# Second batch's first pair turned by the DMA crossbar, fp32 sums ahead of relus, GpSimd casts in another order

## The chip, the cores and the metric

The kernel runs on one NeuronCore of a Trainium2 chip. Five engines work beside each other, each through its own instructions in order: TensorE (PE; its weight loads are listed as PEld), VectorE (DVE), ScalarE (ACT), GpSimd (POOL) and SyncE (SP), which here only starts DMAs. They wait for each other through semaphores. The metric is the device time of one execution in microseconds (us). Before the change it is 285.78 us, the median of four executions from 285.17 to 286.19.

## What is computed

A block-sparse attention over 4 batches of 8 heads, 768 positions and 64 features, and behind it a mixer with a low-rank step over the positions and a two-layer network over the features:

```python
def _attn_ref(q, k, v, sampled_blocks):
    scores = scale * np.matmul(q, k.transpose(0, 1, 3, 2))
    ...                                   # mask: neighbour, edge and sampled blocks of 32
    scores = np.where(mask, scores, -1000000000.0)
    scores = scores - np.max(scores, axis=-1, keepdims=True)
    attn = np.exp(scores)
    attn = attn / (np.sum(attn, axis=-1, keepdims=True) + 1e-09)
    return np.matmul(attn, v).astype(np.float32)

def _moe_ref(x, U, V, w_ch1, w_ch2):
    xt = x.transpose(0, 2, 1)
    h = xt @ U @ V                        # U: 768 x 32, V: 32 x 768
    u = x + h.transpose(0, 2, 1)
    ch = np.maximum(u @ w_ch1, 0.0) @ w_ch2    # 512 x 2048, 2048 x 512
    return (u + ch).astype(np.float32)
```

x is the attention's output with the heads side by side: 4 x 768 x 512.

## The kernel before

**Tiling.** Two heads make a pair, `i` = 0 to 15, four pairs to a batch. Positions are six tiles of 128. A pair's scores are made in nine *units*, `u` = 0 to 8: `scores` (L464) writes one unit into a PSUM tile `psc` of 128 x 1024, ScalarE exponentiates it into `est` (L481), and the values (`pav`) are summed from the nine `est` tiles. Reciprocal and product on VectorE give `xs` (fp32); a cast gives `xh` (fp16). The mixer then makes `pa` from `xh` and U, casts it to `a`, makes `ph` from `a` and V, adds `xs` to get `xf` (fp32), casts that to `uh` (fp16) and turns it into `uT`. The network reads `uT`: `pt` = w1 x `uT`, a relu to `tT` (fp16), `pch` = `tT` x w2, and the sum with `xf` is stored.

**Queries and keys** are loaded by SP in fp32 (`qld`, `kld`), cast by GpSimd to `qst`, `kst` (`cast`, L235), and then turned so that the features lie on the partitions. This is done in one of two ways: by TensorE transposes into a PSUM tile `pturn` and a VectorE copy out of it (`turn_part`, L918), or by a DMA through the crossbar started on SP (`turn_dma`, L261). `qst`, `kst` and the turned `qT`, `kT` have two buffers each.

**The first batch** (pairs 0 to 3) is an order written by hand. The loop at L1025 makes the scores of a unit, then the values of the unit three before it (`flush_value`), then calls `at_unit(i, u)` (L945), which places everything else: loads, casts, the turns of the next pair (`turn_part(i + 1, ...)`), the mask, the weight loads issued by GpSimd (`WLOADS`) and the mixer's steps of the pair before (`tails`). Here the mask is added inside the score product, through one-hot rows in `qa` and `ka`. In pair 0 (L977 to L1005) GpSimd casts U, V and then pair 2's q, k, v.

**From the second batch on** a planner orders the work while the kernel is built. It keeps a clock for each engine (`clk`), lists of due tasks (`later`, `run_engines`) and a list of w1/w2 steps of the batch before (`fill`, `run_fill`); scores are multiplied by a 0/1 mask on VectorE (L502). A relu may go to ScalarE or VectorE, whichever its clocks say is free first. `unit_sides` (L1043) turns pair `i + 1` by the crossbar at unit 0 of pair `i`, for `i` over 4: the crossbar so begins with pair 6.

**The head between the two** (L1078 to L1115) is written out. The first three units of pair 4 are made beside the end of batch 0; their masks wait in `early`. The last pair's `xs` and `xf` in fp32 are put off (`put_off`), so that the fp16 forms that feed `uT` come first. Then come eight short w1 steps, of which five are each followed by `run_engines(1e9)`, which places all due relus; then the fp32 sums; then two more PSUM double tiles are opened (`more_doubles`); then pair 5 is turned by TensorE (L1109 to L1111).

Of the kernel before, what the change touches and what calls it, by code (L numbers as in the profile page):

```python
# [21 lines left out]
def kernel(  # L22
# [12 lines left out]
    nc = tc.nc  # L35

    B, H, S, D = q.shape
    BLK = 32
    NB = S // BLK
    T = S // P  # L40
    HD = H * D
    HP = H // 2
    R = moe_U.shape[1]
# [54 lines left out]
    keep = tc.keep_in_program_order  # L98
# [5 lines left out]
    clk = {"pe": 0.0, "act": 0.0, "dve": 0.0, "pool": 0.0}  # L104
# [30 lines left out]
    def later(eng, first, fn, when=None):  # L135
        count[0] += 1
        when = clk["pe"] if when is None else when
        tasks[eng].append((when + LAG, first, count[0], fn))

    def run_engines(t):  # L140
        while True:
            best = None
            for eng in ("act", "dve"):
                for kind in (eng, "any"):
                    for task in tasks[kind]:
                        start = max(clk[eng], task[0])
                        late = 0.15 if kind == "any" and eng == "dve" else 0.0
                        key = (start + late, task[1], task[2])
                        if start <= t and (best is None or key < best[0]):
                            best = (key, eng, kind, task, start)  # L150
            if best is None:
                return
            _, eng, kind, task, start = best
            tasks[kind].remove(task)
            clk[eng] = start
            clk[eng] += task[3](eng)

    def more_doubles(tag, n):
        first[tag].__exit__(None, None, None)
        pool = ctx.enter_context(  # L160
            tc.tile_pool(
                name=f"double{n}p", bufs=1, space=bass.MemoryType.PSUM,
                side="left" if tag == "ps" else "right",
            )
        )
        doubles[n] = (pool, clk["pe"])
# [38 lines left out]
    Ut = wpool.tile([P, T, P], FP16)  # L205
    Vt = wpool.tile([P, T, P], FP16)
# [22 lines left out]
    def issue(i, names="qkv"):  # L229
        if i >= NPAIR:  # L230
            return
        for nm in names:
            keep(nc.sync.dma_start(out=new_ld(i, nm), in_=src_of(nm, i)))

    def cast(i, nm):  # L235
        if i >= NPAIR:
            return
        b, hp = divmod(i, HP)
        ld = lds.pop((i, nm))
        if nm == "v":  # L240
            keep(
                nc.gpsimd.tensor_copy(  # L242
                    out=vts[b % 2][:, 2 * hp : 2 * hp + 2, :, 0:D], in_=ld
                )
            )
            return
        st = stpool.tile([P, T, 2, D], FP16, tag="st" + nm, name=nm + "st")
        keep(nc.gpsimd.tensor_copy(out=st.rearrange("p t h d -> p h t d"), in_=ld))  # L248
        sts[i, nm] = st
# [11 lines left out]
    def turn_dma(i, nm):  # L261
        if i >= NPAIR:
            return
        st = sts.pop((i, nm))
        qkT[i, nm] = qkpool.tile([P, T, P], FP16, tag=nm + "T", name=nm + "T")
        keep(
            nc.sync.dma_start_transpose(
                out=qkT[i, nm], in_=st.rearrange("p t h d -> p (t h d)")
            )
        )  # L270
# [647 lines left out]
    def turn_part(i, nm, part):  # L918

        if part == 0:  # L920
            turning[nm] = pst_tile([P, T, P], FP16, "pturn", tag="ps")
        turn_some(sts[i, nm], turning[nm], 3 * part, 3 * part + 3)
        if part == 1:
            del sts[i, nm]
            pt = turning.pop(nm)
            if i < HP:
                dst = {"q": qa, "k": ka}[nm][i % 2]
                for h in range(2):
                    half_copy(nc.vector.tensor_copy, dst, h, pt, 0, T)
            else:  # L930
                qkT[i, nm] = qkpool.tile([P, T, P], FP16, tag=nm + "T", name=nm + "T")
                keep(nc.vector.tensor_copy(out=qkT[i, nm], in_=pt))
            run_on("dve", 0.48)
# [8 lines left out]
    }  # L942


    def at_unit(i, u):  # L945
        if (i, u) in MASKS:
            mask_tiles(MASKS.index((i, u)))
        if i == 0:
            if u == 0:
                warm_pe(1)  # L950
                turn_some(qst, pq, TQ, T)
                turn_some(kst, pk, TK, T)
                for h in range(2):
                    mask_rows("dve", h, pm2[:, 0, 0:QB], QA, S)
                    keep(
                        nc.sync.dma_start(
                            out=qa[1][h][mrows[h], :], in_=qa[0][h][mrows[h], :]
                        )
                    )
                    hot_rows(nc.sync, 1, h, D)  # L960
                for nm, o, pt, t in (("q", qa[0], pq, TQ), ("k", ka[0], pk, TK)):
                    for h in range(2):
                        half_copy(nc.vector.tensor_copy, o, h, pt, t, T)
                for h in range(2):
                    keep(nc.sync.dma_start(out=mvld[h * R : h * R + R], in_=moe_V))
                keep(
                    nc.sync.dma_start(
                        out=uld, in_=moe_U.rearrange("(p t) r -> p (t r)", t=T)
                    )
                )  # L970
                issue(2, "qk")
                cast(1, "q")
                cast(1, "k")
                cast(1, "v")
            if u == 1:
                issue(2, "v")
            if u == 3:  # L977
                for r in range(2):
                    at = r * R
                    keep(  # L980
                        nc.gpsimd.tensor_copy(
                            out=Ut[rows[r]].rearrange("p t (h c) -> p t h c", h=2)[
                                :, :, :, at : at + R
                            ],
                            in_=uld[rows[r]]
                            .rearrange("p (t r) -> p t r", t=T)[:, :, None, :]
                            .broadcast_to([D, T, 2, R]),
                        )
                    )
                keep(  # L990
                    nc.gpsimd.tensor_copy(
                        out=Vt[0 : 2 * R, :, :],
                        in_=mvld.rearrange("r (p t) -> r t p", t=T),
                    )
                )
                issue(3)
            if u == 6:
                cast(2, "q")
                cast(2, "k")
                cast(2, "v")  # L1000
            if u == 4:
                turn_part(1, "q", 0)
                turn_part(1, "q", 1)
            if u in (5, 6):
                turn_part(1, "k", u - 5)  # L1005
            return
        if u == 0:
            issue(i + 3)
        if i == 2 and u == 0:
            for h in range(2):  # L1010
                keep(nc.sync.dma_start(out=Vd[rows[h]], in_=Vt[rows[0]]))
        if (i, u) in WLOADS:
            WLOADS[i, u]()
        if u in (1, 2, 3, 4):
            turn_part(i + 1, "qk"[(u - 1) // 2], (u - 1) % 2)
        if u == 6:
            cast(i + 2, "q")
            cast(i + 2, "k")
        if u == 8:
            cast(i + 2, "v")  # L1020
        for _ in range({0: 1, 5: 2, 6: 1, 7: 1}.get(u, 0)):
            if tails:
                tails.popleft()()
# [48 lines left out]
    def run_fill():  # L1072
        cost, fn, kind = fill.popleft()
        fn()
        state["last"] = clk["pe"]
        return cost
# [3 lines left out]
    for gi in range(3):  # L1080
        next_unit(True)
        if gi == 0:
            flush_value()
            tails.popleft()()
            flush_value()
        if gi == 1:
            flush_value()
            put_off.pop(0)()
        if gi == 2:
            tails.popleft()()  # L1090
            tails.popleft()()
            put_off.pop(0)()


    fill.extend(mlp_steps(0))
# [4 lines left out]
    tails.popleft()()  # L1100
    run_fill()
    tails.popleft()()
    for _ in range(5):
        run_fill()
        run_engines(1e9)
    while put_off:
        put_off.pop(0)()
    more_doubles("pav", 2)
    for nm in "qk":  # L1109
        for part in range(2):  # L1110
            turn_part(HP + 1, nm, part)  # L1111
    clk["pe"] = clk["dve"] = max(clk["act"], clk["pe"])
    more_doubles("ps", 3)
    for mask in early:
        later("dve", 3, mask, 0.0)  # L1115

    opened, credit = 1, 0.0
    uT_at = {b: [] for b in range(B)}
# [115 lines left out]
```

## Time and profile before

| what | value |
|---|---|
| median of 4 executions | 285.78 us |
| profiled execution | 285.17 us, its span 283.4 us |
| granted TensorE clock | 0.999 |
| exps on ScalarE (L481) | 144, 142.5 us, 1030 ns each |
| w1 and w2 matmuls | 95.6 and 93.4 us busy |
| mask products on VectorE (L502) | 108, 834 ns each |
| transposes by the crossbar | 12 of uT, 10 of qT, 10 of kT |
| bytes moved by DMA | 37.2 MB, 131 GB/s on average |

The profile is that of one execution on the chip. A row of a timeline gives the start, the duration, the engine, the line and the operation, what it writes and reads, and how many instructions were merged; in brackets stands the idle time before it and what ended it. The duration of matmuls is modelled and contains a latency, so the distance from start to start says what one costs. Times count from the start of the span.

### The profile page before, as it was taken

What the parts mean: (1) busy time and instruction counts of PE and PEld (TensorE: products, weight loads), DVE (VectorE), ACT (ScalarE), POOL (GpSimd) and SP (SyncE); (2) the same over time, 40 slices, a digit from 0 to 9 for tenths busy, and PEclk for the clock granted to TensorE, in tenths of its full rate; (3) what the DMA queues carried; (4) which work ended last, traced back from release to release, by engine and by line L of the source; (5) the groups of instructions that cost most, each with busy time, mean ns of one, the idle gap of its engine ahead of it and who ended that gap; (6) DMA issues with size and microseconds to landing.
All of it is one profiled execution on the core that took longest, in us unless ns stands there. A gap on an engine that the chain in (4) does not pass through costs nothing.

```text
span 283.4 us, 8067 instructions
## 1 busy us (share of the span) xinstructions
PE 275.4 (97%) x3509; PEld 164.9 (58%) x3509; DVE 182.5 (64%) x285; ACT 178.5 (63%) x201; POOL 85.4 (30%) x102
## 2 busy tenths in 40 slices
PE   8999999799999999999999999999999999999996
PEld 3477775456565656656656464656565654565443
DVE  5667767866979898986876959886768551000112
ACT  3799996397969676584894757496868200665000
POOL 2578854103345353341332525151102011000000
PEclk9999999999999999999999999999999999999999
DMA  6999999916264695656154574912100303100112
GB/s 171 275 320 301 238 259 268 251 30 197 56 200 49 191 214 200 137 192 160 41 119 133 124 205 120 169 30 58 30 2 2 102 10 97 75 0 2 74 74 75
DMA packets 45235, 37.20 MB, mean 131 GB/s; under 512 B 27144, under 2 KB 42832, under 8 KB 45200
## 3 DMA queue, kind: packets, MB, share of 16 engines
q1 hardware_dynamic: 42024, 32.26, 41.4%
q0 software_dynamic: 2688, 4.19, 8.0%
q8 instruction: 27, 0.44, 0.7%
q10 hardware_dynamic: 488, 0.24, 0.3%
q14 instruction: 8, 0.07, 0.1%
HBM read 27.90 MB, written 6.29 MB: 121 GB/s over the span
## 4 chain that ended last, share of the span: by engine, by line
PE 83%; ACT 12%; DVE 2%; issue 1%; DVEq 0%
PE pch L174 29%; PE pt L174 29%; ACT est L481 12%; PE pav L174 10%; PE psc L174 9%; PE warm L174 2%; PE pa L174 1%; PE ph L174 1%; PE pturn L254 1%; DVE tT L721 1%; PE pm L174 0%; DVE xh L524 0%; DVE est L502 0%; PE puT L686 0%; DVE uT L695 0%
## 5 line engine op out<-in xcount | busy, mean ns | idle before, releaser
L481 ACT ACTIVATE est<-psc 128x1024 f16<-128x1024 f32 x144 | 142.5, 1030 | 43.9 <-PE psc L174 41.5
L174 PE MATMUL pt<-uT,w1t 64*128 64x384 f16 (+1 forms) x896 | 95.6, 324 | 1.0 <-ACT est L481 0.5
L502 DVE TENSOR_TENSOR est<-est,m 128x1024 f16<-128x1024 f16 x108 | 87.0, 834 | 12.1 <-ACT est L481 11.5
L174 PE MATMUL pch<-w2t,tT 64*128 64x512 f16 (+3 forms) x688 | 93.4, 372 | 0.5 <-ACT est L481 0.5
L174 PEld LDWEIGHTS <-w1t 64*128 64x128 f16 (+1 forms) x896 | 46.6, 95 | 37.3 <-PE pt L174 7.0
L174 PEld LDWEIGHTS <-tT 64*128 64x128 f16 (+1 forms) x688 | 38.4, 95 | 38.3 <-PE pch L174 1.6
L719 ACT ACTIVATE tT<-pt 128x768 f16<-128x768 f32 (+1 forms) x50 | 38.6, 780 | 32.0 <-PE pt L174 31.9
L174 PEld LDWEIGHTS <-est 128*128 128x128 f16 x1152 | 41.4, 97 | 11.0 <-issue 5.0
L174 PE MATMUL pav<-vt,est 128*128 128x65 f16 x1152 | 44.5, 193 | 0.1
L774 DVE TENSOR_TENSOR of<-xf,pch 128x1024 f32<-128x1024 f32 (+3 forms) x16 | 15.2, 953 | 43.4 <-PE pch L174 43.3
L174 PE MATMUL psc<-qT,kT 64*128 64x512 f16 (+1 forms) x288 | 40.7, 324 | 0.0
L581 POOL CAST xh<-xs 128x768 f16<-128x768 f32 x12 | 11.1, 923 | 95.6 <-DVE xs L572 78.5
L667 POOL CAST uh<-xf 128x768 f16<-128x768 f32 x12 | 13.4, 1118 | 32.8 <-DVE xf L658 17.2
L174 PE MATMUL psc<-qa,ka 128*128 128x512 f16 (+1 forms) x96 | 21.9, 331 | 0.2
L174 PEld LDWEIGHTS <-kT 64*128 64x128 f16 x288 | 14.5, 94 | 11.0 <-DVE xs L572 0.2
L721 DVE TENSOR_SCALAR tT<-pt 128x768 f16<-128x768 f32 (+1 forms) x18 | 16.3, 910 | 5.2 <-PE pt L174 5.2
L242 POOL CAST vt<-vld 128x768 f16<-128x768 f32 x16 | 17.3, 1082 | 4.1 <-DMA vld<-in_v_dram 4.1
L248 POOL CAST kst<-kld 128x768 f16<-128x768 f32 x15 | 15.1, 1009 | 2.2 <-PE ph L174 1.6
L248 POOL CAST qst<-qld 128x768 f16<-128x768 f32 x15 | 15.2, 1012 | 1.5 <-DMA qld<-in_q_dram 1.4
L658 DVE TENSOR_TENSOR xf<-xs,ph 128x768 f32<-128x768 f32 x12 | 11.4, 953 | 2.3 <-PE ph L174 2.0
L572 DVE TENSOR_TENSOR xs<-pav,rcp 128x768 f32<-128x768 f32 x12 | 11.5, 958 | 1.2
L570 DVE RECIPROCAL rcp<-pav 128x12 f32<-128x12 f32 x12 | 2.8, 232 | 12.8 <-PE pav L174 12.8
(65 smaller groups left out, 127.3 us busy)
## 6 DMA issues: line engine op xcount, KB each, us to landing
vld<-in_v_dram SPq DMA_DIRECT2D x16, 384.0 KB, 5.6
qld<-in_q_dram SPq DMA_DIRECT2D x15, 384.0 KB, 4.4
kld<-in_k_dram SPq DMA_DIRECT2D x15, 384.0 KB, 5.5
out_dram<-of SPq DMA_DIRECT2D x9, 512.0 KB, 3.1
w1t<-in_moe_w_ch_dram POOLq DMA_DIRECT2D x4, 512.0 KB, 9.8
w2t<-in_moe_w_ch_dram POOLq DMA_DIRECT2D x4, 512.0 KB, 17.8
out_dram<-of SPq DMA_DIRECT2D x5, 256.0 KB, 2.0
qld<-in_q_dram SPq DMA_DIRECT2D x1, 256.0 KB, 2.9
```

The costliest lines, as they stand in the source:

```text
L174: ins = nc.tensor.matmul(out, lhsT, rhs, start=start, stop=stop, skip_group_check=loose)
L242: nc.gpsimd.tensor_copy(out=vts[b % 2][:, 2 * hp : 2 * hp + 2, :, 0:D], in_=ld)
L248: keep(nc.gpsimd.tensor_copy(out=st.rearrange("p t h d -> p h t d"), in_=ld))
L481: keep(nc.scalar.activation(out=est, in_=psc, func=AF.Exp, scale=0.125))
L502: keep(nc.vector.tensor_tensor(out=o, in0=o, in1=m, op=ALU.mult))
L572: nc.vector.tensor_tensor(out=xs.rearrange("p (c j) (h d) -> p c (j h) d", c=2, h=2), in0=pv[:, :, :, 0:D], in1=rcp[:, :, :, None].broadca ...
L581: keep(nc.gpsimd.tensor_copy(out=xh, in_=xs))
L658: nc.vector.tensor_tensor(out=u.rearrange("p (c j) n -> p c j n", c=2), in0=xs.rearrange("p (c j) n -> p c j n", c=2), in1=ph[:, :, 0:HS]. ...
L667: keep(nc.gpsimd.tensor_copy(out=uh, in_=u))
L719: keep(nc.scalar.activation(out=o, in_=i, func=AF.Relu))
L721: keep(nc.vector.tensor_scalar_max(out=o, in0=i, scalar1=0.0))
L774: nc.vector.tensor_add(out=of, in0=xfs[b][:, sc : sc + nsc, n0:n1], in1=pch)
```

## The change

It has four parts.

1. *Pair 5 is turned by the crossbar.* `turn_dma(HP + 1, "q")` and `"k"` are called after the third unit of pair 4; the twelve TensorE transposes and two VectorE copies in the head are gone.
2. *The head's order.* After four of the eight w1 steps the clocks of ScalarE and VectorE are set, the fp32 sums and the early masks are placed, and then the last four w1 steps run. The relus are placed when the planner goes on and no longer between the steps. With the clocks so set, the first two relu pairs both go to ScalarE. Before, one pair went to each. The planner's order of units and steps after it changes in places in the second and third batches' stages.
3. *Turns in the first batch.* Pair 1's key is turned wholly in unit 6 of pair 0 (before: halves in units 5 and 6). Pair 2 is turned in units 2 to 5 of pair 1 (before: 1 to 4).
4. *GpSimd's order.* `cast_U` moves from unit 3 to unit 6 of pair 0; V's cast and pair 2's v cast move to unit 2 of pair 1. In GpSimd's own order this puts both behind pair 2's q and k casts and behind the two `xh` casts of pair 0.

```diff
@@ -942,6 +942,28 @@
     }
 
 
+    def cast_U():
+        for r in range(2):
+            at = r * R
+            keep(
+                nc.gpsimd.tensor_copy(
+                    out=Ut[rows[r]].rearrange("p t (h c) -> p t h c", h=2)[
+                        :, :, :, at : at + R
+                    ],
+                    in_=uld[rows[r]]
+                    .rearrange("p (t r) -> p t r", t=T)[:, :, None, :]
+                    .broadcast_to([D, T, 2, R]),
+                )
+            )
+
+    def cast_V():
+        keep(
+            nc.gpsimd.tensor_copy(
+                out=Vt[0 : 2 * R, :, :],
+                in_=mvld.rearrange("r (p t) -> r t p", t=T),
+            )
+        )
+
     def at_unit(i, u):
         if (i, u) in MASKS:
             mask_tiles(MASKS.index((i, u)))
@@ -975,44 +997,31 @@
             if u == 1:
                 issue(2, "v")
             if u == 3:
-                for r in range(2):
-                    at = r * R
-                    keep(
-                        nc.gpsimd.tensor_copy(
-                            out=Ut[rows[r]].rearrange("p t (h c) -> p t h c", h=2)[
-                                :, :, :, at : at + R
-                            ],
-                            in_=uld[rows[r]]
-                            .rearrange("p (t r) -> p t r", t=T)[:, :, None, :]
-                            .broadcast_to([D, T, 2, R]),
-                        )
-                    )
-                keep(
-                    nc.gpsimd.tensor_copy(
-                        out=Vt[0 : 2 * R, :, :],
-                        in_=mvld.rearrange("r (p t) -> r t p", t=T),
-                    )
-                )
                 issue(3)
             if u == 6:
+                cast_U()
                 cast(2, "q")
                 cast(2, "k")
-                cast(2, "v")
             if u == 4:
                 turn_part(1, "q", 0)
                 turn_part(1, "q", 1)
-            if u in (5, 6):
-                turn_part(1, "k", u - 5)
+            if u == 6:
+                turn_part(1, "k", 0)
+                turn_part(1, "k", 1)
             return
         if u == 0:
             issue(i + 3)
+        if i == 1 and u == 2:
+            cast_V()
+            cast(2, "v")
         if i == 2 and u == 0:
             for h in range(2):
                 keep(nc.sync.dma_start(out=Vd[rows[h]], in_=Vt[rows[0]]))
         if (i, u) in WLOADS:
             WLOADS[i, u]()
-        if u in (1, 2, 3, 4):
-            turn_part(i + 1, "qk"[(u - 1) // 2], (u - 1) % 2)
+        at = u - 2 if i == 1 else u - 1
+        if at in range(4):
+            turn_part(i + 1, "qk"[at // 2], at % 2)
         if u == 6:
             cast(i + 2, "q")
             cast(i + 2, "k")
@@ -1090,6 +1099,8 @@
             tails.popleft()()
             tails.popleft()()
             put_off.pop(0)()
+            turn_dma(HP + 1, "q")
+            turn_dma(HP + 1, "k")
 
 
     fill.extend(mlp_steps(0))
@@ -1100,19 +1111,18 @@
     tails.popleft()()
     run_fill()
     tails.popleft()()
-    for _ in range(5):
-        run_fill()
-        run_engines(1e9)
+    run_fill()
+    clk["act"] = clk["pe"]
+    clk["dve"] = clk["pe"] + 0.5
     while put_off:
         put_off.pop(0)()
-    more_doubles("pav", 2)
-    for nm in "qk":
-        for part in range(2):
-            turn_part(HP + 1, nm, part)
-    clk["pe"] = clk["dve"] = max(clk["act"], clk["pe"])
-    more_doubles("ps", 3)
     for mask in early:
         later("dve", 3, mask, 0.0)
+    for _ in range(4):
+        run_fill()
+    more_doubles("pav", 2)
+    more_doubles("ps", 3)
+    run_engines(clk["pe"])
 
     opened, credit = 1, 0.0
     uT_at = {b: [] for b in range(B)}
```

## The prediction

> **What bounds the kernel now.** I read the page's busy line, then busy time by windows, then the waits and the orders in time around the edits.
>
> ```profile
> PE 275.4 (97%) x3509; PEld 164.9 (58%) x3509; DVE 182.5 (64%) x285; ACT 178.5 (63%) x201; POOL 85.4 (30%) x102
> ```
>
> ```profile
> 20.00:30.00 10.00, 9.89 (x154) 7.54 (x151) 7.81 (x18) 9.99 (x12) 7.98 (x14) 1.00 1.06 299
> 40.00:50.00 10.00, 9.31 (x129) 5.86 (x127) 6.74 (x17) 7.22 (x9) 3.66 (x6) 1.00 1.16 268
> 50.00:60.00 10.00, 8.35 (x98) 4.62 (x96) 7.70 (x14) 6.08 (x10) 0.83 (x1) 1.00 0.71 169
> ```
>
> The windows' columns are length, then PE, PEld, DVE, ACT and POOL busy, granted clock, DMA share, GB/s. TensorE is full nearly everywhere; its worst stretch is 50 to 60 us, the head of the second batch, with 1.65 us idle. From 20 to 30 us ScalarE is as full as TensorE. So there are three stages: the first batch, to 45 us, paced by ScalarE and TensorE together; the head; and the rest, where a TensorE microsecond is worth about one at the end.
>
> **The head: the gain.** Its order in time (start, duration, engine, instruction, and in brackets the idle time before it and its releaser):
>
> ```profile
> 49.65 1.46 PE L174 MATMUL pt<-uT,w1t 64*128 64x384 f16 x14
> 50.92 0.87 ACT L719 ACTIVATE tT<-pt 128x384 f16<-128x384 f32 x2 [1.55 <-PE pt L174]
> 51.15 1.02 DVE L721 TENSOR_SCALAR tT<-pt 128x384 f16<-128x384 f32 x2 [1.04 <-PE pt L174]
> 52.09 1.01 DVE L628 TENSOR_TENSOR xf<-xs,ph 128x384 f32<-128x384 f32 x2
> 52.69 0.51 PE L254 MATMUL pturn<-id,qst 128*128 128x128 f16 x6 [1.58 <-DVE xf L628]
> 53.60 0.82 PE L174 MATMUL pt<-uT,w1t 64*128 64x384 f16 x8
> 54.79 1.02 ACT L481 ACTIVATE est<-psc 128x1024 f16<-128x1024 f32 x1 [3.00 <-PE psc L174]
> ```
>
> TensorE ends at 51.11, waits 1.58 for the first fp32 sum to free a PSUM tile (VectorE does two relus before it), turns pair 5 (q, k: 12 transposes, 52.69 to 53.60 = 0.91) and goes on with w1. The change takes out the turns and their two VectorE copies (0.56 and 0.55), puts the sums at about 50.12 (right behind the uT copy) and gives both relu pairs to ScalarE. TensorE's next w1 half waits only for VectorE's uT copy (ended 50.11) and starts at about 50.9: 53.60 - 50.9 = 2.7 us earlier.
>
> Some goes back, as ScalarE's queue is now longer. Row by row, with a w1 half of 8 matmuls at 0.65 (54.53 to 55.83 holds two), scores at 0.22, exp at 0.96, a relu pair at 0.83, results ready 0.2 after issue: the ScalarE order is relus 50.92 to 52.6, exp to 53.6, exp to 54.5, the relu pair of the next w1 tile to 55.4. The third scores need that last tile's PSUM: TensorE is there at 54.6 and stops 0.8. After that nothing stops it again up to pair 5's first scores, which come at 50.9 + 12 halves x 0.65 + 6 scores x 0.22 + 0.24 (one pair of halves back to back) + 0.83 = 61.1. In the profile they are at 61.79, with 10 halves done; the two more are worth 1.30. Gain: 61.79 - 61.1 + 1.30 = **2.0 us**. Ends: 2.7 if ScalarE stops nothing, 1.0 if its longer queue stops TensorE again.
>
> **The first batch: the loss.** ScalarE runs 36 exps without a gap, 0.951 each:
>
> ```profile
> 10.72 34.23 ACT L481 ACTIVATE est<-psc 128x1024 f16<-128x1024 f32 x36 [0.16 <-PE psc L174]
> ```
>
> Nothing can be won here. Scores are ready 0.65 after they start (0.60 and a signal), so TensorE may be some 0.3 late (0.951 - 0.65) before ScalarE feels it. Three edits touch this:
>
> Both halves of pair 1's key turn in one unit: 0.43 scores + 0.25 values + 0.33 turns = 1.01 in that unit, 0.06 over an exp: hidden by the 0.3; bare it costs 0.1.
>
> Pair 2's turns a unit later put its two key copies on VectorE (1.12, from 23.25) ahead of the cast of the mixer's sum a, which starts at 24.35 and not 23.57. TensorE's ph matmuls wait for a (23.91 to 24.7), and the next scores start at 24.86, not 24.08: 0.45 past the 0.3.
>
> GpSimd's order is the dear one. Before:
>
> ```profile
> 16.86 1.55 POOL L991 CAST Vt<-w2t 64x768 f16<-64x768 f32 x1
> 20.67 0.98 POOL L542 CAST xh<-xs 128x384 f16<-128x384 f32 x2
> 21.59 1.22 POOL L421 DMA_DIRECT2D w1t<-in_moe_w_ch_dram  x2
> 22.80 0.84 POOL L248 CAST qst<-qld 128x768 f16<-128x768 f32 x1
> 24.90 0.51 POOL L642 CAST uh<-xf 128x384 f16<-128x384 f32 x1 [0.49 <-DVE xf L628]
> 25.87 0.52 POOL L642 CAST uh<-xf 128x384 f16<-128x384 f32 x1
> ```
>
> ```profile
> 26.75 0.50 PE L694 MATMUL puT<-id,uh 128*128 128x128 f16 x6
> ```
>
> The change puts Vt and pair 2's v cast behind both xh casts. The second xh waits for its xs (21.08 on VectorE), so GpSimd idles early and then has in a row: 21.1 + 0.46 (xh) + 1.50 (Vt) + 0.77 (v) + 1.21 (two w1 loads issued) + 2 x 0.77 (q, k) + 0.45 (uh) + 0.52 (w1 load) + 0.5 (uh) = 28.0. uh's second half was done at 26.39; TensorE's puT transposes want it at 26.9. They wait 1.1, the next scores start at 28.2 and not 27.08, are ready at 28.85, and their exp was due at 27.84. Loss: **1.0 us**. The 0.45 above lies inside it: the second delay is fixed by GpSimd's clock. What else is queued there (w1 loads 2.4 later, pair 3's casts 2.3 later, done 26.6, wanted 27.76) stays covered; w1 has ten microseconds to spare. Ends: 0.3 (GpSimd back within its slack), 1.3 (both delays partly add).
>
> **The crossbar: cover, and a rule against it.** SP issues pair 5's two transposes (1.32 and 1.22 in the rows) behind pair 7's q load, at 39.9 and about 41.3; pair 7's k load behind them goes from 40.25 to some 43 and is first used by a cast at 70.44. They land when the DMA engines let them:
>
> ```profile
> q0 software_dynamic: 1540, 1.53, 64.4%
> q1 hardware_dynamic: 1535, 2.18, 50.6%
> ```
>
> These are the packets from 38 to 52 us: weights on q0, pair loads and transposes on q1. The row for free engines (75.8) says 2.8 us to landing: in at 46, hidden. The Trainium skill ("DMA: Bandwidth & Descriptors", Anatomy of one DMA, Arbitration) says each engine takes turns between queues packet by packet. The counts agree, 1540 to 1535, a pair each 0.146 us per engine, and loads in this stage take 13.3 and 15.1 to land instead of some 4.5. By that rule the transposes stand behind pair 7's q load (39.48 + 13.3 = 52.8) and have 96 packets per engine, 0.02 each alone (0.93 us for 48 at 75.5), but one weight packet (0.082) between each two while weights last, to some 56.4: 36 packets by then, the other 60 in 1.2: 57.6; with w1 begun 2.4 later, about 59. The scores want them at 61.1 + 1.0 = 62.1. I take the rule's value; it too is hidden. Ends: nothing, and 3 us late (the slower rival).
>
> **The rest.** The same work follows; the order of units and w1/w2 steps shifts in batches 0 and 1 and is the old one at the end. TensorE's stops there after 62 us come to some 2 us (0.47 at 95.9, 0.25 at 68.2 and such); I take as many after, half a microsecond either way.
>
> **Sum.** -2.0 + 1.0 = -1.0 on the profiled execution: 285.17 (span 283.4 and 1.77 around it) to 284.2. That execution was the fastest of the four, 0.6 below their median, so 285.78 becomes 284.8.
>
> **Rivals.**
> *The first batch loses nothing* (ScalarE absorbs it, GpSimd goes faster): 285.78 - 2.0 = 283.8. For it: GpSimd idles 0.49 at 24.4. Against: uh had only 0.5 to spare and gets 1.6 later.
> *ScalarE binds at the head*: gain 1.0 of the 2.7, eaten by the first batch: 285.8. For it: it gets two relus (0.87) and has no gap from 50.9 on. Against: it also gets back 3.00 of idling.
> *Slower: the crossbar comes late.* If the weights, started 2.4 later, last through all 96 packets, the transposes land at 52.8 + 2.4 + 96 x 0.10 = 64.8, 2.7 after the scores want them, and TensorE stands in order: 284.8 + 2.7 = 287.5. It decides from a landing at about 64 on. For it: the DMA share is over 1 from 24 to 55 us. Against: the engines go idle at 56.4 before; two transposes add 1.9 us to a fixed backlog.
>
> **Chances.** A measurement tells 0.3% (0.86 us) from no change. Forecast 0.46 (two thirds of its spread below 284.92), no loss 0.22, ScalarE 0.16, crossbar 0.16. Faster 0.30 + 0.21 = 0.51; same 0.16 + 0.13 = 0.29; slower 0.20. The range, 283.2 to 286.8, leaves out most of the crossbar case and a little below.
>
> **What would show it.** Head: no pturn at 50 to 54, ScalarE from relus into exps without the 3.00 gap, TensorE idle under 1 us from 50 to 60. First batch: the exps broken once, by about 1 us, before the second or third exp of pair 2, with puT waiting for GpSimd's uh. Crossbar: qT and kT take over 12 us to land, and no scores wait for them. If the exps run on unbroken, or kT's landing releases TensorE, I am wrong at that step.

## The result, and the profile after

The changed kernel takes 285.03 us (median of 43 executions, 283.92 to 287.06), the kernel before, measured beside it, 285.93 (64 executions, 285.05 to 288.52). The ratio is 0.9962, its 95% interval 0.9949 to 0.9974: about 1.1 us faster (285.93 x 0.0038), the interval 0.7 to 1.5. The medians differ by 0.90 and the means (286.19 and 285.10) by 1.09: the kernel before takes over 287 us in 12 of its 64 executions, the changed one in 1 of 43. The two *profiled* executions say the opposite: 285.17 before (one of the fastest, span 283.4) and 285.69 after (span 283.9). How both can be true is half of what follows.

The three windows that answer to those shown before (length, then PE, PEld, DVE, ACT and POOL busy, clock, DMA share, GB/s), after the change; the third window is new, and its row from before stands ahead of them:

```profile
110.00:120.00 10.00, 10.00 (x164) 6.10 (x160) 8.93 (x12) 7.21 (x8) 4.24 (x4) 1.00 0.65 155
```

```profile
20.00:30.00 10.00, 8.49 (x122) 6.17 (x120) 6.24 (x14) 8.07 (x10) 9.43 (x14) 1.00 0.95 283
50.00:60.00 10.00, 9.94 (x118) 4.95 (x112) 7.39 (x12) 7.64 (x14) 1.89 (x2) 1.00 1.29 193
110.00:120.00 10.00, 8.53 (x130) 5.08 (x127) 9.15 (x13) 6.99 (x8) 4.14 (x4) 1.00 0.45 64
```

The head has improved: TensorE was busy for 8.35 us of 50 to 60 and is now for 9.94. Two other places pay. In the first batch ScalarE loses 1.92 us (9.99 to 8.07). At 110 us, where TensorE had been busy for all 10.00 us, 1.47 are now missing, 60 us behind the last edit.

**The head**, in order of time, after (start, duration, engine, instruction, idle time before it and its releaser):

```profile
51.42 2.12 PE L174 MATMUL pt<-uT,w1t 64*128 64x384 f16 x22
51.80 1.01 DVE L628 TENSOR_TENSOR xf<-xs,ph 128x384 f32<-128x384 f32 x2
52.69 1.64 ACT L719 ACTIVATE tT<-pt 128x384 f16<-128x384 f32 x4 [1.55 <-PE pt L174]
54.19 1.06 ACT L481 ACTIVATE est<-psc 128x1024 f16<-128x1024 f32 x1
62.20 0.38 PE L174 MATMUL psc<-qT,kT 64*128 64x512 f16 x2
```

The fp32 sums run right behind the uT copy, w1 goes on without the stop of 1.58, four relu halves pass on ScalarE, the exp follows at once (before: after a gap of 3.00). Pair 5's first scores start at 62.20 and wait for nothing.

To compare heads without the first batch, I count from a landmark, pair 3's first `pa` matmul on TensorE, before and after:

```profile
45.91 0.33 PE L174 MATMUL pa<-xh,Ut 128*128 128x128 f16 x3 [0.17 <-DVE xh L524]
```

```profile
47.69 0.33 PE L174 MATMUL pa<-xh,Ut 128*128 128x128 f16 x3 [0.18 <-DVE xh L524]
```

From there to pair 5's first scores it took 61.79 - 45.91 = 15.88, and takes 62.20 - 47.69 = 14.51 with two more w1 halves done (1.31): the head gains 15.88 + 1.31 - 14.51 = **2.68**. From there to the end of the span it took 237.49 and takes 236.21: 1.28 of the 2.68 remain. The landmark itself is 1.78 later. So -1.28 + 1.78 = +0.5 for these two executions: that is the 0.52 between 285.17 and 285.69.

**The wait at 110 to 120**, TensorE, after:

```profile
116.32 0.66 PE L174 MATMUL pt<-uT,w1t 64*128 64x384 f16 x6 [0.25 <-ACT est L481]
118.20 0.34 PE L174 MATMUL pt<-uT,w1t 64*128 64x384 f16 x2 [1.22 <-DMA uT<-uh]
118.47 2.46 PE L174 MATMUL pav<-vt,est 128*128 128x65 f16 x72
```

The two idle times make 1.47; 1.22 of it is a wait for `uT`, the 0.25 ahead of it one for an exp. In the new planner's order the next batch's w1 begins before a unit of values (72 matmuls, 2.4 us); before, it came behind them:

```profile
117.40 2.46 PE L174 MATMUL pav<-vt,est 128*128 128x65 f16 x72
119.79 0.82 PE L174 MATMUL pt<-uT,w1t 64*128 64x384 f16 x8
```

In the changed kernel `uT` isn't there yet: GpSimd casts `uh` from 114.16 to 115.33, SP starts the transpose at 115.35, it lands at 118.2.

**The first batch**: the exps of ScalarE, after. Before, all 36 ran in one row from 10.72.

```profile
9.44 15.40 ACT L481 ACTIVATE est<-psc 128x1024 f16<-128x1024 f32 x16 [1.70 <-PE psc L174]
25.34 2.94 ACT L481 ACTIVATE est<-psc 128x1024 f16<-128x1024 f32 x3 [0.51 <-PE psc L174]
29.56 17.17 ACT L481 ACTIVATE est<-psc 128x1024 f16<-128x1024 f32 x18 [1.28 <-PE psc L174]
```

Two gaps, 0.51 and 1.28. What TensorE waits for just ahead of each, and two GpSimd rows that stand behind the second:

```profile
24.49 0.33 PE L174 MATMUL ph<-a,Vt 128*128 128x128 f16 x3 [0.53 <-POOL vt L242]
28.69 0.34 PE L694 MATMUL puT<-id,uh 128*128 128x128 f16 x3 [0.64 <-POOL uh L642]
```

```profile
20.43 0.83 POOL L248 CAST kst<-kld 128x768 f16<-128x768 f32 x1 [1.55 <-DMA kld<-in_k_dram]
28.12 0.52 POOL L642 CAST uh<-xf 128x384 f16<-128x384 f32 x1
```

The first names GpSimd's v cast (ended 24.44), but VectorE's cast of `a` ended at 24.43 too; with the turns alone changed (below) the same 0.53 is put down to `a`. The second is the late `uh`. It is later here than GpSimd's own work makes it: the cast of pair 2's key waited for its load until 20.43, and the two `xh` casts, V's cast and all behind them stood in order behind it. Where that load is in time (the first-batch-only run below), V's cast starts at 21.40 and not 22.11.

**The crossbar**: SP's queue, after.

```profile
41.68 7.87 SPq L267 DMA_TRANSPOSE qT<-qst  x1
49.65 5.17 SPq L267 DMA_TRANSPOSE kT<-kst  x1
54.88 0.58 SPq L233 DMA_DIRECT2D kld<-in_k_dram  x1
```

Each transpose holds SP here, where the DMA engines are full (share 1.29 from 50 to 60), 13 us for the two, and pair 7's k load behind them starts at 54.88 instead of 40.25. Nobody waits for it. qT landed 18.6 us after its issue, at 60.3.

### The profile page after: what moved, and what is told of

Its sections match the earlier page's. It is cut to its first block, busy times and chain, and to the rows that moved or that the text cites. A ratio compares the mean times of both kernels' runs of the same rounds, so it can differ in the third digit from the quotient of the medians.

```text
span 283.9 us, 8041 instructions
## 1 busy us (share of the span) xinstructions
PE 274.8 (97%) x3497; PEld 164.4 (58%) x3497; DVE 178.5 (63%) x281; ACT 179.1 (63%) x203; POOL 84.7 (30%) x102
## 4 chain that ended last, share of the span: by engine, by line
PE 80%; DMA 7%; ACT 5%; issue 3%; POOL 2%; DVE 1%; SPq 0%; ACTq 0%; POOLq 0%; DVEq 0%
PE pt L174 30%; PE pch L174 28%; PE pav L174 10%; PE psc L174 8%; ACT est L481 5%; DMA kld<-in_k_dram 3%; DMA vld<-in_v_dram 3%; PE pa L174 2%; DMA uT<-uh 1%; PE ph L174 1%; POOL w1t L421 1%; POOL kst L248 0%; DVE xh L524 0%; POOL uh L642 0%; POOL xh L542 0%
## 5 line engine op out<-in xcount | busy, mean ns | idle before, releaser
L502 DVE TENSOR_TENSOR est<-est,m 128x1024 f16<-128x1024 f16 x108 | 84.7, 808 | 15.4 <-ACT est L481 15.0
L174 PEld LDWEIGHTS <-tT 64*128 64x128 f16 (+1 forms) x688 | 39.0, 95 | 37.0 <-PE pch L174 0.9
L719 ACT ACTIVATE tT<-pt 128x768 f16<-128x768 f32 (+1 forms) x52 | 39.2, 769 | 32.6 <-PE pt L174 32.6
L721 DVE TENSOR_SCALAR tT<-pt 128x768 f16<-128x768 f32 x16 | 15.3, 955 | 4.6 <-PE pt L174 4.6
L242 POOL CAST vt<-vld 128x768 f16<-128x768 f32 x16 | 16.6, 1039 | 4.3 <-DMA vld<-in_v_dram 4.3
L248 POOL CAST kst<-kld 128x768 f16<-128x768 f32 x15 | 14.2, 948 | 4.6 <-DMA kld<-in_k_dram 4.6
L174 PEld LDWEIGHTS <-ka 128*128 128x128 f16 (+1 forms) x108 | 8.8, 97 | 3.8 <-issue 2.3
```

Of the source, the lines that this page charges most:

```text
L174: ins = nc.tensor.matmul(out, lhsT, rhs, start=start, stop=stop, skip_group_check=loose)
L242: nc.gpsimd.tensor_copy(out=vts[b % 2][:, 2 * hp : 2 * hp + 2, :, 0:D], in_=ld)
L502: keep(nc.vector.tensor_tensor(out=o, in0=o, in1=m, op=ALU.mult))
L719: keep(nc.scalar.activation(out=o, in_=i, func=AF.Relu))
L721: keep(nc.vector.tensor_scalar_max(out=o, in0=i, scalar1=0.0))
```

## The experiments

Numbers named "landmark to end" are span minus the landmark's start, 237.49 before and 236.21 after. Kernels that are alike behind the landmark agree in it to about 0.1: four with the old head have 237.41 to 237.49, three with the changed head 236.19 to 236.23. The labels in brackets (e1 to e11) are those that the expectations use.

### Which part brings the gain

(e1) Parts 1 and 2 alone (the crossbar and the head's order), so with the first batch's edits taken back from the changed kernel:

```diff
-                cast_U()
...
-        if i == 1 and u == 2:
-            cast_V()
-            cast(2, "v")
...
-        at = u - 2 if i == 1 else u - 1
+        if u in (1, 2, 3, 4):
```

(e2) Parts 3 and 4 alone, with the head's edits taken back:

```diff
-            turn_dma(HP + 1, "q")
-            turn_dma(HP + 1, "k")
...
-    clk["act"] = clk["pe"]
-    clk["dve"] = clk["pe"] + 0.5
```

> The head's two edits alone (crossbar turn of pair 5, new order of sums and relus), first batch as before. Theory A (the first batch loses 1.0 to 1.8 us, which the head's gain pays for): 1.0 to 1.8 us faster than the full change, so 1.9 to 2.7 us below the kernel before, ratio 0.990 to 0.9935; exps of the first batch unbroken; if uT lands late at the start of batch 1's w1, 1.5 of the head's 2.65 is lost again and the ratio is at the upper end. Rival B (the first batch's edits cost nothing at the end, the head gains only 0.9): the same as the full change, ratio 0.996.

> The first batch's edits alone (turns a unit later, GpSimd's order), head as before. Theory A: slower by 1.0 to 1.8 us, ratio 1.0035 to 1.0065, with one or two gaps of 0.5 to 1.3 us in the exps between 24 and 30 us. Rival B: ratio 1.000 within 0.001.

Head only: 284.32 us (22 executions), ratio 0.996 (0.9939 to 0.9982), landmark to end 236.19, with the wait for `uT` in it (1.21 on TensorE, behind 0.25 for an exp). First batch only: 285.97 (14; the kernel before, beside it, 285.59), ratio 1.000 (0.9977 to 1.0024), landmark to end 237.41, and two gaps in the exps:

```profile
25.42 2.94 ACT L481 ACTIVATE est<-psc 128x1024 f16<-128x1024 f32 x3 [0.51 <-PE psc L174]
28.86 17.17 ACT L481 ACTIVATE est<-psc 128x1024 f16<-128x1024 f32 x18 [0.50 <-PE psc L174]
```

So the whole gain is the head's. Of the microsecond that the first batch loses in these rows the ratio shows nothing and the medians 0.4. My theory, a head worth 2 to 3 us and a first batch that costs 1 to 2, missed on both.

### The two halves of the first batch

(e3) The GpSimd casts alone, on the kernel before:

```diff
             if u == 6:
+                cast_U()
                 cast(2, "q")
                 cast(2, "k")
-                cast(2, "v")
...
+        if i == 1 and u == 2:
+            cast_V()
+            cast(2, "v")
```

(e4) The turns alone, on the kernel before (and pair 1's key turned in one unit, as in the change):

```diff
+        at = u - 2 if i == 1 else u - 1
+        if at in range(4):
+            turn_part(i + 1, "qk"[at // 2], at % 2)
```

> GpSimd's order of casts alone, turns and head as before. Theory A with uh as the cause: TensorE's puT waits for uh's second half, one gap of about 1.0 us in the exps, slower by 0.8 to 1.3 us, ratio 1.003 to 1.0045; ph may also wait for Vt. Rival (the turns' shift is what delays the first batch): no gap over 0.3 us, ratio 1.000.

> The turns a unit later alone, GpSimd's order and head as before. Theory A: the cast of a starts 0.8 later on VectorE, ph waits, one gap of at most 0.45 us in the exps near 25 us; ratio 1.000 to 1.0016. Rival (the shift costs the whole loss): 1.0 us or more, ratio over 1.0035.

Casts: 286.35 (14; before beside it 285.59), ratio 1.0009 (0.9987 to 1.0032), the gap of 1.28 with the wait for `uh` 0.63, and one of 0.91 behind a late query load. Turns: 285.73 (14), ratio 0.9999 (0.9976 to 1.0023), the gap of 0.51, with `ph` waiting 0.53 for `a`, and one of 1.65 where TensorE waits for `qst`. So each edit makes a gap of its own. Together they don't simply add: in the four profiled executions with both edits the gaps sum to 1.01 (first batch only), 1.18, 1.77 and 1.79. The 1.79 is the changed kernel's, with the late key load. In the 1.01 GpSimd's chain was not held by a load; there the first gap delays TensorE and so shortens its wait for `uh` (0.3).

Yet the ratios stay at 1. The reason is in what the old order does in other executions than the one I had. In the head-only run the first batch is that of before, and its exps are broken by 2.25 us:

```profile
17.90 1.07 POOL L981 CAST Ut<-w2t 64x384 f16<-64x384 f32 x2 [2.52 <-DMA w2t<-in_moe_U_dram]
19.03 1.53 POOL L991 CAST Vt<-w2t 64x768 f16<-64x768 f32 x1
20.50 0.83 POOL L248 CAST qst<-qld 128x768 f16<-128x768 f32 x1
```

```profile
21.38 0.34 PE L254 MATMUL pturn<-id,qst 128*128 128x128 f16 x3 [2.38 <-POOL qst L248]
```

U landed at 17.90; in the profile of before its cast started at 15.73. GpSimd stands behind that load in order, and V's cast of 1.53 behind it, ahead of the query cast that TensorE turns next. The changed order takes V's cast out of this chain, so a late U costs it less. A late U is not even needed: with the turns alone its cast began at 15.93, but ScalarE's exps had begun 1.4 us earlier (8.10) and the turn waited 1.78. The landmark shows how far the profiled executions lie apart: with the old first batch 45.91, 49.41, 47.33, 46.62, 46.96, 48.54 (mean 47.5, spread 3.5), with the new one 47.69, 46.99, 46.40, 47.37 (mean 47.1, spread 1.3); e3 and e4, with one half of the new one each, have 46.15 and 45.78. These are few, and the means are not told apart. The execution that I had worked from was the earliest of the six.

The two latest, 49.41 and 48.54, lost time twice. TensorE stood there for 2.38 and 3.19 us, and when it had been working again for about 1.2 us its granted clock went to 0.50 and stayed there for some 3.4 us. The window of head only that answers to those shown before has a mean clock of 0.83:

```profile
20.00:30.00 10.00, 8.62 (x105) 6.43 (x106) 4.64 (x10) 6.63 (x7) 8.17 (x14) 0.83 1.01 293
```

That alone makes the mean clock of the whole execution 0.994 (3.4 x 0.5 is 0.6% of 285.6), and this mean is known of many executions that were not profiled. It is 0.993 or 0.994 in 25 of 149 executions of kernels with GpSimd's old order, and in 1 of 101 with the new one; in all others it is 0.998 or more. Beside e1 to e4 the kernel before has 8 such executions of 51, at 287.1 us in the mean; its other 43 have a median of 285.4, against 285.97 of the first batch alone. So by these medians (14 executions of the latter) an ordinary execution does lose some 0.5 us by the new first batch, and the long stops with the lowered clock, which the new order nearly always avoids, bring the ratio back to 1. That all 25 had such a stop is inferred: two of them were profiled.

### Crossbar and order apart

(e5) The crossbar with the old order of the head, against the kernel before:

```diff
             put_off.pop(0)()
+            turn_dma(HP + 1, "q")
+            turn_dma(HP + 1, "k")
...
-    for nm in "qk":
-        for part in range(2):
-            turn_part(HP + 1, nm, part)
```

(e6) The new order with the turns left on TensorE, against the changed kernel without parts 3 and 4:

```diff
-            turn_dma(HP + 1, "q")
-            turn_dma(HP + 1, "k")
...
     more_doubles("pav", 2)
+    for nm in "qk":
+        for part in range(2):
+            turn_part(HP + 1, nm, part)
```

> Of the head only the crossbar turn of pair 5; relus before the fp32 sums as before, first batch as before. Measured from the last pair's mixer sum (pa, where TensorE waits 0.17 for xh: 45.91 before, 47.69 after the full change) to the end of the span: 237.49 before, 236.21 after. Theory: the 0.91 of turns goes, but TensorE now meets the late sums at the first scores of the head instead; 1.2 gained, 236.3; the later order is that of before, so no uT wait at 118 us. Rival (the sums' wait was bound to the turns' PSUM tile alone): 2.5 gained, 235.0.

> Of the head only the order (sums ahead of relus, both first relu pairs to ScalarE), pair 5 still turned by TensorE; first batch as before. From pa to the end: theory: the 1.58 wait before the turns goes, but the planner's later order is that of the full change and loses about 1.5 to the uT wait near 118 us; 237.2 to 237.5, nothing gained. Rival (the uT wait has another cause than the planner's order): no uT wait, 235.9.

One execution each. Crossbar only: 286.08 us, landmark to end 236.97, 0.5 less than before where 1.2 less was expected. Its first scores of the head wait 1.39 for the fp32 sum, as the turns did before them. And the slower rival's mechanism shows itself, in small:

```profile
62.30 0.10 PEld L174 LDWEIGHTS <-kT 64*128 64x128 f16 x2 [0.48 <-DMA kT<-kst]
```

Order only: 285.22, landmark to end 236.78, 0.7 less, better than the 0 to 0.3 expected. Pair 5's first scores come 15.55 behind the landmark (62.17 - 46.62): the order alone gains 15.88 + 1.31 - 15.55 = 1.64 of the 2.68, the crossbar the other 1.04 (the turns were 0.91). It has the wait for `uT` too (1.16, behind 0.25 for an exp), so that wait comes from the order and not from the crossbar.

### The wait for uT

(e7) Head only, with the planner told that `uT` comes 4.0 us after the cast instead of 3.0:

```diff
-            then(run_on("pool", 1.15, end) + 3.0)
+            then(run_on("pool", 1.15, end) + 4.0)
```

> Head as in the full change, first batch as before, and the planner told that a turned uT is there 4.0 instead of 3.0 us after its cast, so that batch 1's w1 begins one value step later. Theory: the uT wait of 1.47 near 118 us goes and the head's whole 2.65 stands; from pa to the end 234.7 to 235.0. Rival (what is saved there is lost to other stalls of the new order): 236.2.

284.23 us, landmark to end 235.44 against 236.19: 0.75 gained in this one execution, between the theory and the rival, with no wait for `uT` from 110 to 125. TensorE still stops there for 0.25 (an exp) and 0.22 (the product `xs`). So the wait for `uT` is on the path, and part of its 1.22 is replaced when it is taken away.

### A head that keeps the old order behind it

(e8) The crossbar as above, and the fp32 sums popped ahead of the five w1 steps; the rest of the head, its relus between the steps and its clocks, as before:

```diff
     tails.popleft()()
+    while put_off:
+        put_off.pop(0)()
     for _ in range(5):
         run_fill()
         run_engines(1e9)
-    while put_off:
-        put_off.pop(0)()
     more_doubles("pav", 2)
```

> Crossbar turn of pair 5 and the fp32 sums straight behind the uT copy, but the relus placed between the w1 steps as before, so that one pair goes to each engine and the planner's later order is that of before; first batch as before. Theory: both 0.91 and 1.58 are gained and no uT wait comes: from pa to the end 234.8 to 235.1, ratio to before 0.990 to 0.9925. Rival (the order of before holds other stalls that eat it): 236.2, ratio 0.996.

284.73 us (13, lowest 283.16), ratio 0.9944 (0.9916 to 0.9972), landmark to end 235.16, near to the 234.8 to 235.1 of the theory: 1.05 better there than the change, with no wait of TensorE for `uT` at 110 to 124. The relus are split between ScalarE and VectorE as before the change, and no loss from it shows in the head: the gain is that the sums come first. What else the change writes anew there (the clocks set by hand, the relus put off, the masks ahead of the last steps) gives the planner another order later, and that order is the worse one. Which of these does it was not tried apart.

By the ratio the gain is less than the theory's (0.990 to 0.9925), though the interval reaches into that range. The first batch, the old one, again stood for `qst`, 3.19 in the profile, and 4 of the 13 executions have the lowered clock. So (e9) the casts of U and V were taken out of GpSimd's chain and given to VectorE, on top of this head (the first line below in both functions):

```diff
-                nc.gpsimd.tensor_copy(
+                nc.vector.tensor_copy(
...
     def at_unit(i, u):
+        if (i, u) == (0, 7):
+            cast_V()
+        if (i, u) == (1, 0):
+            cast_U()
```

> The head of e8 and, in the first batch, U's and V's casts on VectorE (V after unit 7 of pair 0, U after the first unit of pair 1) instead of GpSimd; turns as before. Theory C (in the old order the gaps of up to 3 us in the exps near 20 us come from U's load: its cast stands in GpSimd's queue ahead of pair 2's q and k casts, and U lands between 15.3 and 17.9 us): no wait of a turn for GpSimd's qst, no wait of puT for uh, exps unbroken after pair 0's start-up; faster than e10 by 0.5 to 1.5 us, ratio to before 0.986 to 0.992. Rival (the gap comes from q's own load landing late): the turn waits for qst as in e8.

283.46 us (6, lowest 282.4), ratio 0.9909 (0.9875 to 0.9942): the best of all. One of the six, 287.92 at a clock of 0.994, is not in the ratio, though such executions of the kernel before are; with it the means stand at 0.993. From 9.54 on its exps have one gap, where the two casts on VectorE (1.18 and 1.08) delay the product `xs`:

```profile
9.54 12.49 ACT L481 ACTIVATE est<-psc 128x1024 f16<-128x1024 f32 x13 [1.80 <-PE psc L174]
22.67 22.93 ACT L481 ACTIVATE est<-psc 128x1024 f16<-128x1024 f32 x24 [0.63 <-PE psc L174]
```

(e10, e11) The same head with the change's own first batch, and the whole change once more beside it:

> The head of e8 with the full change's first batch (its turns and GpSimd's order). Theory C: the first batch of the change trades the wait for qst (0 to 3.2 us, with U's landing) for waits of ph and puT (1.0 to 1.8 us, nearly always), so in the median it is as fast as e8: ratio to before 0.993 to 0.9955; from pa to the end 235.1 to 235.3. Rival A (it costs 1.0 to 1.8 against the old order): ratio 0.998.

> The full change itself, on the chip and beside the runs of e9 and e10. Theory C: 1.0 to 1.3 us slower than e10, which has its first batch but no uT wait near 118 us: ratio to before 0.996 to 0.998. Rival (the uT wait costs nothing at the end): the same as e10.

The whole change: 285.21 (22), ratio 0.997 (0.9952 to 0.9987), landmark to end 236.23, as at first. The other: 284.2 (7), ratio 0.994 (0.9917 to 0.9963), but landmark to end 236.2 where 235.1 to 235.3 was expected. So the ratio came as expected, and not for the reason given. The weight loads of TensorE say why:

```profile
60.71 0.10 PEld L174 LDWEIGHTS <-kT 64*128 64x128 f16 x2 [1.36 <-DMA kT<-kst]
```

Pair 5's keys landed at 60.7. In this order its first scores were due 13.2 us behind the landmark, at 59.6; in the whole change one more w1 tile lies ahead and they are due at 14.5. That extra tile is what covers the crossbar. It also spoils the comparison of first batches that e9 and e10 were meant to be: in the profiles e9 is 1.06 shorter from the landmark on, where the keys waited in e10, and its landmark is no earlier (46.56 against 46.40). What casting U and V on VectorE is worth is not shown.

## Why the prediction came out right

The forecast was a gain of 1.0 us in all, median 284.8; it is 1.1 by the ratio, and 285.03. By the medians it is 0.9. That the sum is right is luck: three of its terms are off, the head by 0.7 in one direction, the first batch by 1.0 in the same and the rest by 1.4 in the other.

| step | predicted | measured |
|---|---|---|
| head | -2.0 | -2.68 (landmark to pair 5's scores) |
| the rest | 0, give or take 0.5 | +1.40 (2.68 - 1.28; near 118 us TensorE stops for 1.47, of which 1.22 is the wait for `uT`) |
| first batch | +1.0 | in the exps +1.01 alone, +1.79 in the changed kernel's profile; 0 by the ratio (1.000, 0.9977 to 1.0024), 0.4 by the medians |
| crossbar | hidden, landing at about 59 | hidden; qT at 60.3, kT about 60.9 |

**Head.** The mechanism held in each row named: no turns, no gap of 3.00, TensorE idle 0.06 us from 50 to 60. The term that was mis-sized is the 0.8 given back at the third scores: ScalarE's longer queue stopped TensorE nowhere. Its four relus took 1.64 in a row, and the exps behind them came in time. The outer end, 2.7, was the value.

**The rest** is where the prediction failed. It said that the order of later units shifts, read the stops of the old order (some 2 us) and took as many after. But the rewritten head gave the planner's clocks and lists another start, so another order came out, and that order asks for `uT` one step before it can be there. The instruction order of the changed kernel shows w1 ahead of the values; the rows of before show a transpose's landing (75.8: 2.8) and what the cast takes. The wait could have been computed.

**First batch.** Place and mechanism held (`puT` waits for `uh`; the second half ended at 28.64, wanted at about 28.05). Where GpSimd's chain ran free of loads, in the first-batch-only run, even the size held: `uh`'s second half ended at 27.95 against the 28.0 of the sum, and the gaps make 1.01, so that there the 0.45 did lie inside. What failed is that the loss was taken from one execution as if it were the kernel's. In that one U landed early, and the old order's weakness, V's cast between U and the query cast, didn't show. In other executions the old order stands up to 3.2 us there, and loses more after it by the lowered clock. Moving the result from the profiled execution to the median by the constant 0.6 assumed that both orders vary alike.

**Crossbar.** The landing at about 59, reckoned by the Trainium skill's rule that each engine takes turns between queues packet by packet ("DMA: Bandwidth & Descriptors"; the paragraph stands in the section on queues, rings and completion order, not in the one that the prediction names), is near to what came: 60.3 for qT. The row for free engines (2.8 to landing, in at 46) would have been 14 us off. The cover was thinner than I said, though: in the kernel with the sums first and the change's first batch kT was issued 0.23 earlier (49.42) and released its scores at 60.71; that makes about 60.9 in the whole change, an estimate from that run, against scores that load kT at 62.03: 1.1 us to spare. In two kernels with one tile less ahead of them it was gone (0.48, 1.36). Not foreseen at all was that SP would be held; it did no harm.

Of the rivals, ScalarE at the head did not occur, the late crossbar did not in this order, and "the first batch loses nothing" is true of the ratio, for a reason that I had not named: not that the new order is free, but that the old one isn't either.

**Still open:** 0.3 to 0.4 us. With the old order behind it, the head that puts the sums first gains 2.69 up to pair 5's scores and 2.33 at the end; the crossbar alone gains 0.90 there (15.88 - 14.98) and 0.52. Where the difference goes was not traced. And the stops of the first batch were seen in ten profiled executions; in the others only the mean clock speaks of them.

## What to carry to other kernels

Before a loss is charged to an order of instructions, look at how the same stage runs in several executions: where small loads share full DMA engines, a chain that stands in order behind one of them can differ by microseconds from one execution to the next, and one profile shows a single draw. When an edit changes the clocks of a planner, read the order that comes out far behind the edit, and hold each consumer that has moved forward against the landing of what it reads. And take a gain by the smallest edit that gives it: here the sums put first and the crossbar, without the new clocks, were 1 us better from the landmark on than the change, as long as the crossbar's keys came in time.

## What the runs showed of the hardware

- A transpose through the crossbar held its issuing queue for 7.87 and 5.17 us while the DMA engines were full, 9.26 and 5.25 in another run; with free engines it is 1.22. The k load behind them on SP started at 54.88 instead of 40.25.
- The landing of one small load moved by 2.2 us between executions of kernels with the same work ahead of it: U's cast started at 15.73 in one and at 17.90 in another.
- Casting V (64 x 768 from fp32) took 1.18 us on VectorE and 1.51 to 1.58 on GpSimd; U's two casts took 1.08 and 1.06 to 1.07.
- After TensorE had stood for 2.38 us in one execution and 3.19 in another, and worked again for about 1.2, its granted clock was 0.50 for some 3.4 us (mean clock of these executions 0.994). Behind stops of 1.78 and 1.88 us in two others it did not fall (mean clock 1.000).
